# Talking-heads attention and a SoLU layer: scores of two heads on row halves of TensorE's array, the first mixing of two units on its quarters

## The chip, the core and the metric

The kernel runs on one core of a Trainium2 chip. The core has TensorE (PE in the profile; PEld is its loading of weights), VectorE (DVE), ScalarE (ACT), GpSimd (POOL) and SyncE (SP), which here only issues DMAs. The metric is the device time of one execution in microseconds, lower is better. It was 733.37 us as the median of three runs (726.63 to 737.01).

## What is computed

```python
# q, k, v: (4, 12, 448, 64); w_pre, w_post: (12, 12)
scores = q @ k.T / 8                                  # (b, h, i, j)
scores = einsum('bhij,hg->bgij', scores, w_pre)       # first mixing, over the heads
attn = softmax(scores, axis=j)
attn = einsum('bhij,hg->bgij', attn, w_post)          # second mixing
x = (attn @ v).transpose(0, 2, 1, 3).reshape(1792, 768)
h = x @ w_in                                          # (1792, 1024)
out = layernorm(h * softmax(h)) * g_ln @ w_out        # (1792, 768)
```

Every fp32 operand of the scores and of the first mixing is held as two fp16 halves, hi and lo, and three of the four products are summed: hi hi, hi lo and lo hi. The second mixing and the product with v run in fp32.

## The kernel before

**Units and blocks.** One batch has 448 rows of scores for each of 12 heads. They are cut into four blocks of rows: three of 120 rows, which are 12 units, and one of 88 rows, which is 9 units. A unit is ten rows of all heads, so 120 partitions. There are 180 units, 45 for each batch, and 16 blocks.

**Scores (`qk`, L473 to L480).** For each block and head, two matmuls of 448 columns, both over 128 rows of contraction. K lies transposed with hi above lo (`k1`), Q with lo above hi (`q2`), and the first matmul gives lo hi + hi lo at once. The second needs hi hi alone, so a copy `q1` holds the hi half of Q on the right 64 partitions and zeros on the others. `move_hi` (L458) fills it with two DMAs per two pairs of heads, from the transposed tile, and `clear_q1` sets its zeros at the start. `score_hi` on ACT and `score_lo` on DVE take each head's bank out of PSUM as fp16 hi and lo into `s` (two buffers).

**From block to unit (`fetch`, L506).** When all twelve heads of a block are out, one DMA per unit (210 KB) on SP's queue brings ten rows of all heads into the 120 partitions of `sr` (three buffers).

**First mixing (`premix`, L511).** Three matmuls of 120 x 120 x 448 with a block-diagonal weight (`wp_hi` twice, `wp_lo` once) into one of three banks (`m`). Then `rowmax` (DVE, L520), `expo` (ACT, L532), the reciprocal (DVE), `weigh` (POOL, L553), `postmix` (fp32, eight matmul instructions, L561), and `post_out` (ACT, L226) into the ring `p_t`. For each block two groups `av` (L601) of 48 instructions form attn times v, with 64 output columns each, so that two heads go to the two column halves of the array; `x_hi` (ACT) and `x_lo` (DVE) split the result.

**Next batch.** K and Q of batch b+1 are loaded, their maxima taken, split (`pair_hi` mostly on POOL, `pair_lo` on DVE or POOL, L397 to L409) and turned by transposing DMAs (`turn_in`, L411) while batch b is worked on. All of it lands on the same engines and on SP's queue.

**Order.** `Plan` is a list scheduler that runs when the program is built. Each task has an engine, a cost, a due time and rings of buffers, and the plan writes the instructions of each engine in one fixed order. On the chip each engine follows its order and waits where an operand is late. Behind attention, from about 486 us on, come the 14 tiles of the SoLU layer, which the change doesn't touch.

## Time and profile before

| | us | share of the span |
|---|---|---|
| median of three runs | 733.37 | |
| shortest, longest run | 726.63, 737.01 | |
| span of the profiled execution | 726.0 | |
| PE busy | 659.8 | 91% |
| DVE busy | 495.6 | 68% |
| ACT busy | 449.7 | 62% |
| POOL busy | 275.4 | 38% |
| premix matmuls (540) | 100.5 + 64.1 | |
| score matmuls (384) | 107.4 | |
| mean granted clock of TensorE | 0.979 | |

The span runs from the first to the last instruction of the profiled execution, and it is 0.6 us below the shortest run. The busy time of a matmul counts it from its start to its end, and matmuls overlap, so how long TensorE needs for a piece of work is read better from the distance between two starts.

### The profile page before, as it was taken

To read this page: it belongs to the slowest core of one execution; us is meant where nothing else is said; L and a number is where in the kernel's file an instruction comes from. 1 tells how busy PE (TensorE), PEld (TensorE's weight loads), DVE (VectorE), ACT (ScalarE), POOL (GpSimd) and SP (SyncE) were. 2 spreads that over 40 slices of the span, in tenths; PEclk is the share of its full clock that TensorE was granted. 3 is DMA by queue.
4 is the path that set the end of the run, shared out by engine and by line. 5 is a ranking of instruction groups with operands and counts; after the bars stand their busy time and mean duration, and the time that the engine had idled before them with its cause. 6 is when DMAs were issued, how large, how long until landed. Compare 5 with 4: busy or idle time off the path is not lost.

```text
span 726.0 us, 14785 instructions
## 1 busy us (share of the span) xinstructions
PE 659.8 (91%) x5206; PEld 479.6 (66%) x5206; DVE 495.6 (68%) x1482; ACT 449.7 (62%) x956; POOL 275.4 (38%) x384
## 2 busy tenths in 40 slices
PE   3487998999997999999999989999998848999998
PEld 2346887888886878877888878774443424566664
DVE  6777996688985778996779999848888764200000
ACT  2567787787786787788788778744555544321111
POOL 6404781134851124771113353603667622320000
PEclk9789999999999999999999999999999989999999
DMA  8736497247577347677256645536456312243112
GB/s 228 121 90 199 136 221 212 84 135 228 180 198 200 87 105 213 199 209 212 95 180 204 212 153 188 139 98 187 121 121 151 68 20 51 51 103 95 44 44 65
DMA packets 121473, 102.47 MB, mean 141 GB/s; under 512 B 75524, under 2 KB 112056, under 8 KB 121400
## 3 DMA queue, kind: packets, MB, share of 16 engines
q1 hardware_dynamic: 115128, 87.07, 43.0%
q0 software_dynamic: 4384, 12.40, 6.4%
q10 hardware_dynamic: 1888, 2.07, 1.0%
q8 instruction: 41, 0.67, 0.4%
q14 instruction: 32, 0.26, 0.1%
HBM read 33.24 MB, written 9.63 MB: 59 GB/s over the span
## 4 chain that ended last, share of the span: by engine, by line
PE 61%; DVE 14%; DMA 11%; POOL 5%; ACT 3%; issue 2%; SPq 2%; DVEq 0%; POOLq 0%; ACTq 0%
PE po L561 15%; PE y L1314 14%; PE pm L515 12%; PE ps L480 9%; PE px L601 8%; DMA sr<-s 7%; PE ps_h L764 3%; DVE cv_wo L699 2%; POOL wo L702 2%; DVE cv_wo L694 1%; DMA raw_q<-in_q_dram 1%; DVE u L1257 1%; DVE wi L222 1%; DVE wo_l L222 1%; DMA q<-q 1%
## 5 line engine op out<-in xcount | busy, mean ns | idle before, releaser
L561 PEld LDWEIGHTS po<-wr,e 120*112 120x112 f32 x1440 | 173.5, 177 | 19.0 <-POOL wr L553 6.3
L561 PE MATMUL po<-wr,e 120*112 120x120 f32 x1440 | 178.6, 267 | 2.9 <-POOL wr L553 2.8
L553 POOL TENSOR_SCALAR wr<-wq,sm 120x120 f32<-120x120 f32 x180 | 78.0, 434 | 257.6 <-DVE sm L549 117.3
L532 ACT ACTIVATE e<-pm,nb,c_exp 120x448 f32<-120x448 f32 x180 | 131.4, 731 | 15.0 <-DVE e L520 9.5
L520 DVE TENSOR_SCALAR_CACHE_REDUCE e<-pm,c_nexp 120x448 f32<-120x448 f32 x180 | 121.2, 676 | 22.2 <-PE pm L515 12.5
L491 DVE SCALAR_TENSOR_TENSOR s<-ps,s 120x448 f16<-120x448 f32 (+1 forms) x192 | 116.9, 618 | 20.3 <-ACT s L486 17.9
L226 ACT COPY p_t<-po 112x480 f32<-112x480 f32 x180 | 104.0, 578 | 32.8 <-PE po L561 31.3
L486 ACT ACTIVATE s<-ps 120x448 f16<-120x448 f32 (+1 forms) x192 | 104.0, 548 | 28.1 <-PE ps L480 20.7
L515 PE MATMUL pm<-sr,wp_hi 120*120 120x448 f16 x360 | 100.5, 361 | 17.9 <-DMA sr<-s 16.8
L480 PE MATMUL ps<-k,q 128*120 128x448 f16 (+1 forms) x384 | 107.4, 366 | 7.8 <-DVE s L491 3.5
L764 PE MATMUL ps_h<-wi,xf 128*128 128x512 f16 x396 | 87.5, 379 | 3.7 <-DVE u L1257 3.6
L1314 PE MATMUL y<-wo_h,lth 128*128 128x384 f16 (+2 forms) x224 | 72.7, 331 | 9.9 <-ACT wo_h L217 9.9
L601 PE MATMUL px<-p_t,raw_v 112*64 112x120 f32 (+1 forms) x1536 | 80.7, 261 | 0.0
L601 PEld LDWEIGHTS px<-p_t,raw_v 112*64 112x64 f32 x1536 | 73.8, 137 | 8.7 <-issue 3.1
L1314 PE MATMUL y<-wo_l,lth 128*128 128x384 f16 (+2 forms) x224 | 72.7, 331 | 2.5 <-DVE wo_l L222 2.0
L1314 PEld LDWEIGHTS <-lth 128*128 128x128 f16 x448 | 44.3, 99 | 43.9 <-issue 15.3
L1314 PE MATMUL y<-wo_h,ltl 128*128 128x384 f16 (+2 forms) x224 | 72.8, 331 | 0.0
L764 PEld LDWEIGHTS <-xf 128*128 128x128 f16 x396 | 38.5, 98 | 49.2 <-issue 4.5
L515 PEld LDWEIGHTS <-wp_hi 120*120 120x120 f16 x360 | 43.2, 134 | 34.4 <-DMA sr<-s 19.9
L480 PEld LDWEIGHTS <-q 128*120 128x120 f16 (+1 forms) x384 | 47.8, 134 | 26.7 <-issue 10.4
L515 PE MATMUL pm<-sr,wp_lo 120*120 120x448 f16 x180 | 64.1, 356 | 0.0
L1322 ACT ACTIVATE o<-y,c_out 128x384 f32<-128x384 f32 (+2 forms) x28 | 16.1, 578 | 72.4 <-PE y L1314 72.4
(168 smaller groups left out, 820.6 us busy)
## 6 DMA issues: line engine op xcount, KB each, us to landing
sr<-s SPq DMA_DIRECT2D x180, 210.0 KB
cv_wi<-in_moe_w_in_dram SPq DMA_DIRECT2D x24, 256.0 KB
cv_wo<-in_moe_w_out_dram SPq DMA_DIRECT2D x8, 768.0 KB
raw_k<-in_k_dram POOLq DMA_DIRECT2D x18, 224.0 KB, 4.4
raw_q<-in_q_dram POOLq DMA_DIRECT2D x18, 224.0 KB, 4.2
raw_v<-in_v_dram POOLq DMA_DIRECT2D x18, 224.0 KB, 3.6
q<-q SPq DMA_DIRECT2D x18, 112.0 KB
xh<-xsh SPq DMA_DIRECT2D x9, 224.0 KB
```

What stands on the lines that cost most here:

```text
L226: nc.scalar.copy(out=out, in_=in_)
L480: nc.tensor.matmul(y, x[:, e, i0 : i0 + n], k1[b, g][:, e], start=(a == 0), stop=(a == 1))
L486: nc.scalar.activation(out=s_t[b, c][0 : y.shape[0], h, 0], in_=y, func=AF.Copy, scale=2.0**-E_S)
L491: nc.vector.scalar_tensor_tensor(out=t[:, h, 1], in0=y, scalar=2.0**-E_S, in1=t[:, h, 0], op0=ALU.mult, op1=ALU.subtract)
L515: nc.tensor.matmul(ps[:, 0:S], w[0:UK], x[:, z], start=(a == 0), stop=(a == 2))
L520: nc.vector.tensor_scalar(out=e, in0=pmx[b, u][:, 0:S], scalar1=c_nexp[0:UK, b : b + 1], scalar2=None, op0=ALU.mult, op1=ALU.min, accum_ou ...
L532: nc.scalar.activation(out=ee[b, u], in_=pmx.pop((b, u))[:, 0:S], func=AF.Exp, bias=nbs.pop((b, u)), scale=c_exp[0:UK, b : b + 1], accum_o ...
L553: ENG[eng].tensor_scalar(out=w, in0=wq[0:UK, 0 : H * UN], scalar1=sums.pop((b, u)), scalar2=1.0, op0=ALU.mult, op1=ALU.mult)
L561: nc.tensor.matmul(ps[:, c * 120 : (c + 1) * 120], e[:, c * CP : (c + 1) * CP], w, start=True, stop=True)
L601: nc.tensor.matmul(xps[b, blk, g][e * 64 : e * 64 + 64, i, 0:n], raws["v", b][:, h, c * D : (c + 1) * D], block_view(b, blk, c * H + h), s ...
L764: nc.tensor.matmul(ps[:, n], xx[:, kc, o : o + 128], ww[:, kc, n * 512 : (n + 1) * 512], start=(kc == 0 and a == 0), stop=(kc == KDM - 1 a ...
L1314: nc.tensor.matmul(y, xx[:, kc], ww[:, kc, cut], start=(kc == 0 and a == 0), stop=(kc == KFF - 1 and a == 2),)
```

## The change

Scores are now made for two heads at a time. The fp16 halves are laid out by pairs: both heads' hi (128 columns) and both heads' lo, so that after the transpose one head lies on partitions 0 to 63 and the other on 64 to 127. Six matmuls of 64 rows, three for each head in turn, write two banks. `q1`, `clear_q1` and `move_hi` are gone. A block's matmuls give 128 rows now, and `fetch` picks its 120 or 88 from them. `pair_lo` on DVE is two instructions of 256 elements in place of one of 512.

The first mixing takes two units at a time. `sr` has room for both, on partitions 4 to 123, so that five rows of each unit lie on either half. Twelve matmuls of 64 x 64 write two banks: bank j gets the j-th half of both units. Where a block has nine units the last goes alone, with three matmuls as before. There are three `sr` buffers for two units each. The weights lie in 128 columns, with four partitions of zeros ahead, and all tiles behind have 128 partitions. `post_out` puts the rows back in order by its access pattern.

```diff
-    def qk(b, c, h):
-        i0, n = ROW0[b][c], ROWS[b][c]
-        for a, x in enumerate((q2[b, g], q1[g])):
-            nc.tensor.matmul(y, x[:, e, i0 : i0 + n], k1[b, g][:, e], start=(a == 0), stop=(a == 1))
+    def qk(b, c, p):
...
+        for a, (x, z) in enumerate(((0, 0), (0, 1), (1, 0))):
+            for e in range(2):
+                w = slice(64 * e, 64 * e + 64)
+                nc.tensor.matmul(
+                    sps[b, c, 2 * p + e],
+                    q2[b, g][w, j, x, i0 : i0 + QCH],
+                    k1[b, g][w, j, z],
+                    start=(a == 0),
+                    stop=(a == 2),
+                )
...
     def premix(b, u):
-        ps = pmx[b, u] = ps_m.tile([UK, 512], F32, tag="m", name=f"pm_{b}_{u}")
-        x = sr[b, u]
+        x, us = sr[b, u], mates(b, u)
+        ps = [ps_m.tile([UK, 512], F32, tag="m", name=f"pm_{b}_{n}")[:, 0:S] for n in us]
         for a, (w, z) in enumerate(((wp_hi, 0), (wp_hi, 1), (wp_lo, 0))):
-            nc.tensor.matmul(ps[:, 0:S], w[0:UK], x[:, z], start=(a == 0), stop=(a == 2))
...
+            for i in range(2):
+                for j in range(2):
+                    q, m = slice(64 * j, 64 * j + 64 - K0 * j), slice(64 * i, 64 * i + 64)
+                    nc.tensor.matmul(ps[j][m], w[q, 0, m], x[q, i, z], **kw)
...
-                        add(
-                            ("q1", b, p),
-                            one(move_hi, b, p, m),
-                            {"act": 0.1 * m} if z else {"sp": 0.6 * m},
...
-                        ring="o" if spare(b, c, h) else "s",
-                        until=[("sl", b, c, h)],
+                            ring="o" if spare(b, c, p) else "s",
+                            until=[[("sl", b, c, h + e)] for e in range(2)],
+                            slots=2,
...
+        for w in (wp_hi, wp_lo, wq):
+            nc.gpsimd.memset(w, 0.0)
+        for w in srs:
+            nc.gpsimd.memset(w[0:K0], 0.0)
...
         else:
-            split_lo(lo, x, s, hi)
+            for h in range(2):
+                split_lo(lo[:, h], x[:, h], s, hi[:, h])
```

**TensorE, second batch, units 4 and 5.** Before (ps are scores, pm the first mixing, po the second, the first number of a name is the batch):

```order
L561 MATMUL po_1_0_2121<-wr_1_0_2040,e_1_0_1994 112x120 x4
L480 LDWEIGHTS q_1_2_1463
L480 MATMUL ps_1_1_8_2130<-k_1_2_1446,q_1_2_1463 120x448
L480 LDWEIGHTS q1_2_127
L480 MATMUL ps_1_1_8_2130<-k_1_2_1446,q1_2_127 120x448
L515 LDWEIGHTS wp_hi_71
L515 MATMUL pm_1_4_2136<-sr_1_4_2023,wp_hi_71 120x448
...
L515 LDWEIGHTS wp_lo_72
L515 MATMUL pm_1_4_2136<-sr_1_4_2023,wp_lo_72 120x448
L561 MATMUL po_1_1_2142<-wr_1_1_2067,e_1_1_2021 112x120 x4
```

The same place of the change, where px is attn times v:

```order
L644 MATMUL px_0_3_0_2249<-p_t_129,raw_v0_261 64x120 x24
L491 LDWEIGHTS q_1_1_1508
L491 MATMUL ps_1_1_6_2290<-k_1_1_1498,q_1_1_1508 128x448
L491 LDWEIGHTS q_1_1_1508
L491 MATMUL ps_1_1_7_2291<-k_1_1_1498,q_1_1_1508 128x448
...
L552 LDWEIGHTS wp_hi_96
L552 MATMUL pm_1_4_2299<-sr1_94,wp_hi_96 64x448
L552 LDWEIGHTS wp_hi_96
L552 MATMUL pm_1_5_2300<-sr1_94,wp_hi_96 64x448
...
L598 MATMUL po_1_1_2318<-wr_1_1_2279,e_1_1_2185 112x120 x4
L598 MATMUL po_1_2_2327<-wr_1_2_2283,e_1_2_2228 112x120 x4
```

Six score matmuls of two heads and twelve of the first mixing of two units now stand together, and two second mixings follow each other. The places where one matmul has another tile shape (whole array, column halves, row halves, quarters) than the one before it rise from 64 to 330 in the whole program.

**SyncE's queue at the end of the first batch.** Before (sr are fetches, k and q the transposes, q1 the moves of `move_hi`):

```order
L419 DMA_TRANSPOSE q_1_1_1326<-hl_q1_1103 128x16x112
L419 DMA_TRANSPOSE k_1_1_1355<-hl_k1_886 128x16x112
L509 DMA sr_0_28_1378<-s_0_2_736 120x1x896
L509 DMA sr_0_29_1393<-s_0_2_736 120x1x896
L464 DMA q1_1_126<-q_1_1_1326 64x896 x2
L419 DMA_TRANSPOSE k_1_2_1446<-hl_k1_886 128x16x112
L509 DMA sr_0_30_1457<-s_0_2_736 120x1x896
L419 DMA_TRANSPOSE q_1_2_1463<-hl_q1_1103 128x16x112
L509 DMA sr_0_31_1482<-s_0_2_736 120x1x896
L509 DMA sr_0_32_1491<-s_0_2_736 120x1x896
L464 DMA q1_2_127<-q_1_2_1463 64x896 x2
L509 DMA sr_0_33_1535<-s_0_3_1145 120x1x896
```

And with the change:

```order
L529 DMA sr0_93<-s_0_2_818 120x1x896 x2
L529 DMA sr1_94<-s_0_2_818 120x1x896 x2
L436 DMA_TRANSPOSE k_1_1_1498<-hl_k1_899 128x16x112
L436 DMA_TRANSPOSE q_1_1_1508<-hl_q1_1160 128x16x112
L436 DMA_TRANSPOSE k_1_2_1578<-hl_k1_899 128x16x112
L436 DMA_TRANSPOSE q_1_2_1594<-hl_q1_1160 128x16x112
L529 DMA sr2_95<-s_0_3_1240 120x1x896 x2
```

The moves are gone, the last fetches of block 2 stand ahead of the last four transposes, and those follow each other without a fetch between.

**GpSimd at the start.** Before:

```order
L296 AFFINE_SELECT mk_118<-mk_118 128x10 x2
masks.py:197 MEMSET ident_70 128x128
masks.py:199 AFFINE_SELECT ident_70<-ident_70 128x128
L456 MEMSET q1_0_125 128x1792
L1131 CAST ident32_69<-ident_70 128x128
L456 MEMSET q1_1_126 128x1792
```

And with the change:

```order
L305 AFFINE_SELECT mk_121<-mk_121 128x10 x2
L314 TENSOR_TENSOR mk5_122<-mk_121 128x5
L316 MEMSET wp_hi_96 128x256
L316 MEMSET wp_lo_97 128x256
L316 MEMSET wq_98 128x128
L318 MEMSET sr0_93 4x1792
L318 MEMSET sr1_94 4x1792
L318 MEMSET sr2_95 4x1792
masks.py:197 MEMSET ident_70 128x128
masks.py:199 AFFINE_SELECT ident_70<-ident_70 128x128
L1168 CAST ident32_69<-ident_70 128x128
```

The clearing of the zeros now stands ahead of the identity matrices, of which `ident32` is an operand of the first maximum over partitions.

## Rows read from the trace of the kernel before

**Rows 1.** Page, part 4: the chain that ended last, by engine
```profile
PE 61%; DVE 14%; DMA 11%; POOL 5%; ACT 3%; issue 2%; SPq 2%; DVEq 0%; POOLq 0%; ACTq 0%
```

**Rows 2.** Windows by block: stretch, length, busy PE, PEld, DVE, ACT, POOL, clock, DMA
```profile
66.50:93.36 26.86, 26.25 (x257) 22.41 (x257) 25.47 (x90) 21.86 (x52) 18.97 (x32) 1.00 0.48 155
...
151.19:179.28 28.09, 26.80 (x255) 23.18 (x254) 23.69 (x83) 21.77 (x51) 12.47 (x24) 1.00 0.62 194
...
206.42:240.56 34.14, 29.93 (x258) 24.45 (x257) 22.18 (x75) 24.77 (x60) 8.07 (x14) 0.95 0.76 196
...
369.94:396.67 26.73, 26.73 (x254) 23.09 (x253) 23.39 (x73) 22.82 (x51) 7.90 (x13) 1.00 0.61 199
...
426.61:455.12 28.51, 26.83 (x250) 22.23 (x249) 26.93 (x80) 23.06 (x52) 12.83 (x15) 1.00 0.61 195
...
sum 439.23, PE 415.91 PEld 348.98 DVE 360.44 ACT 341.62 POOL 180.79; mean PE 25.99 PEld 21.81 DVE 22.53 ACT 21.35 POOL 11.30
```

**Rows 3.** Timeline of PE: start, time, line, operation, shape, count
```profile
143.33 0.54 PE L515 MATMUL pm<-sr,wp_hi 120*120 120x448 f16 x2
...
143.90 0.98 PE L561 MATMUL po<-wr,e 120*112 120x120 f32 x8
144.72 0.54 PE L480 MATMUL ps<-k,q 128*120 128x448 f16 x2
145.10 0.98 PE L561 MATMUL po<-wr,e 120*112 120x120 f32 x8
...
157.07 0.54 PE L480 MATMUL ps<-k,q 128*120 128x448 f16 x2
157.54 2.68 PE L601 MATMUL px<-p_t,raw_v 112*64 112x120 f32 x48
160.15 0.59 PE L480 MATMUL ps<-k,q 128*120 128x448 f16 x2
```

**Rows 4.** Groups by line and form: DVE's splits and its score step
```profile
L491 DVE SCALAR_TENSOR_TENSOR s<-ps,s 120x448 f16<-120x448 f32 x144 | 87.7, 618 | 10.2 <-ACT s L486 8.8 <-DMA sr<-s 0.2
...
L222 DVE SCALAR_TENSOR_TENSOR xsl<-px,x_sc,xsh 128x120 f16<-128x120 f32 x72 | 20.1, 333 | 14.6 <-ACT xsh L217 14.4
...
L222 DVE SCALAR_TENSOR_TENSOR hl_q<-raw_q,p_q,hl_q 112x512 f16<-112x512 f32 x20 | 15.6, 788 | 0.2 <-ACT hl_q L217 0.2
```

**Rows 5.** Chain in order of time, start of the program: start, time, what
```profile
25.77 4.08 DMA q<-hl_q
29.93 6.37 DMA q<-q
36.34 3.92 PE ps L480 x11
42.78 3.85 DMA sr<-s
...
58.74 7.71 DMA sr<-s
```

**Rows 6.** Timeline of SP's queue at the start: the last transpose of Q
```profile
29.92 1.69 SPq L419 DMA_TRANSPOSE q<-hl_q  x1
```

**Rows 7.** Timeline, second batch boundary: SP's queue and the PE behind it
```profile
227.41 2.04 SPq L464 DMA_DIRECT2D q<-q  x2
...
229.50 1.64 SPq L419 DMA_TRANSPOSE q<-hl_q  x1
...
231.24 1.78 SPq L509 DMA_DIRECT2D sr<-s  x2
...
234.11 0.88 PE L515 MATMUL pm<-sr,wp_hi 120*120 120x448 f16 x2 [3.76 <-DMA sr<-s]
```

**Rows 8.** Waits, longest in total: us, times, longest
```profile
PE pm L515 <- DMA sr<-s: 16.8, 14, 3.8
```

**Rows 9.** Timeline, GpSimd at the start and the first use of `ident32`
```profile
4.01 1.59 POOL L456 MEMSET q<- 128x1792 f16 x1
...
5.54 0.29 POOL L1131 CAST ident<-ident 128x128 f32<-128x128 f16 x1
...
9.64 0.77 PE L189 MATMUL spread_k<-ident,amx_k 128*128 128x128 f32 x2 [9.64 <-DVE amx_k L210]
```

More of the change, by code (lines that the diff above doesn't have):

```diff
@@ L29, in __init__, with add @@
         self.tasks = {}
-    def add(self, key, run, on, after=(), behind=(), due=0.0, ring=None, until=(), lat=0.0):
+        self.slots = {}
+    def add(self, key, run, on, after=(), behind=(), due=0.0, ring=None, until=(), lat=0.0, slots=None):
+        if slots:
+            self.slots[key] = slots
         self.tasks[key] = (run, on, list(after), due, ring, list(until), lat, list(behind))
@@ L279 @@
     mk = const.tile([128, UN], F32, name="mk")
+    mk5 = const.tile([128, HN], F32, name="mk5")
     am_w = const.tile([128, 2], F32, name="am_w")
@@ L795, in add_tasks @@
             last = ("mix", i)
-        for g in range(NPAIR // GP):
-            add(("cl", g), one(clear_q1, g), {"pool": 1.6}, due=3.0 + g)
         turns = ([(p, GP) for p in range(0, NPAIR, GP)], [(0, 1), (1, 1), (2, 1), (3, 1), (4, 1), (5, 1)])
@@ L956, in add_tasks @@
                     due=d - 2 * STEP,
-                    ring="sr",
-                    until=[("m",) + g],
+                    ring="sr" if u == mates(b, u)[0] else None,
+                    until=[M(b, u)],
                     lat=2.7,
                 )
-                add(
-                    ("m",) + g,
-                    one(premix, *g),
-                    {"pe": 0.56},
-                    after=[("f",) + g, last] + behind("m"),
-                    due=d,
-                    ring="m",
-                    until=[("ex",) + g],
-                )
+                us = mates(b, u)
+                if u == us[0]:
+                    add(
+                        ("m",) + g,
+                        one(premix, *g),
+                        {"pe": 0.66},
+                        after=[("f", b, n) for n in us] + [last] + [M(*p) for p in [prev] if u or b],
+                        due=d,
+                        ring="m",
+                        until=[[("ex", b, n)] for n in us],
+                        slots=len(us),
+                    )
                 add(
@@ L1053, in add_tasks @@
                         {"sp": 0.65},
-                        after=[("xl", b, NBLK[b] - 1, g) for g in range(NXG)] + [("m", b + 1, 8 + i)],
+                        after=[("xl", b, NBLK[b] - 1, g) for g in range(NXG)] + [M(b + 1, 8 + i)],
                         due=at(b + 1, 10 + i),
@@ L1065, in add_tasks @@
                 {"sp": 0.65},
-                after=[("xd", b, j) for b in range(2) for j in range(XP)] + [("m", o, 28 + 2 * i)],
+                after=[("xd", b, j) for b in range(2) for j in range(XP)] + [M(o, 28 + 2 * i)],
                 behind=[("x0", i - 1)] if i else [],
```

176 lines of the change are left out of this document (99 added, 77 removed).

## The prediction

> **What bounds the kernel now.** The chain that ended last comes first: TensorE holds 61% of it, DVE 14%, DMA 11% [rows 1]. The change touches attention alone, so I cut attention into its 16 blocks, each from its first `premix` to that of the next: together 439.2 us for 180 units, 2.44 us a unit [rows 2]. The reader is to see two kinds of block there. In most, PE is busy nearly throughout and DVE and ACT for some 80 to 85% (151.19, 369.94). In five of them, 60 units, of which 66.50 and 426.61 are the first and the last, DVE is busy for 94% and more (25.47 of 26.86, 26.93 of 28.51): there the split of the next K and Q, or of the weights of the last layer, fills it.
>
> How long TensorE needs is read from the distance of two starts [rows 3]. From 143.33 to 143.90 three premix matmuls take 0.57 us, 0.19 each. From 143.90 to 144.72 a postmix takes 0.82. From 144.72 to 145.10 one head's scores take 0.38. A group of `av` takes 2.61, from 157.54 to 160.15. A block of 12 units needs 12 x (0.57 + 0.82 + 0.38) + 2 x 2.61 = 26.5 us, and the block at 369.94 took 26.73 [rows 2]. So outside the five, TensorE is the bound.
>
> **Term 1: TensorE's work.** Scores now cost 192 x 0.38 = 73.0 us and premixes 180 x 0.57 = 102.6, together 175.6. After it, two heads are three steps of 448 columns if the two row halves run at once, and two units are three steps if the four quarters do. With 0.19 a step that is 96 x 0.57 + 88 x 0.57 + 4 x 0.57 (units left alone) = 107.2, so 68.4 less. Whether halves and quarters run at once no row shows for rows of the array. For columns one does: 48 instructions of `av` would need 48 x 0.1025 = 4.92 us at the pace of postmix (0.82 / 8, the same 120 columns in fp32), and took 2.61, so two column halves did run together [rows 3]. I take the same for rows.
>
> Against this stands the change of tile shape. The scores at 157.07 are followed by `av` after 0.47 us, where others need 0.38 [rows 3]: entering column halves costs 0.09. Leaving them costs at most 2.61 - 24 x 0.1025 = 0.15. The order has 330 such changes where it had 64. At 0.09 for each of the 266 more, that is 24 us and leaves 44.5, or 0.25 us a unit. Bounds: 179 more entries at 0.09 with a free return leave 52 (0.29 a unit); with 0.15 for each return they leave 25 (0.14 a unit).
>
> The Trainium skill ("TensorE: Matmul & The Clock Gate", Measured speedup vs the span model) speaks against the full overlap: four row tiles of 512 columns gave 3.07x and not 4x. By that a step would take 0.19 x 4 / 3.07 = 0.25 us, an estimate, and TensorE would save 175.6 - (552 steps x 0.25 + 2.3 + 24), some 11 us in place of 44.5. The pair of column halves in this trace reached 4.92 / 2.61 = 1.88 of 2, with the return from them inside that number, so I stay with the row.
>
> **Term 2: what of it reaches the end.** In the five blocks that DVE fills I count nothing. In the other eleven, 120 units, TensorE is the bound until the next engine is: 120 x 0.25 = 30 us. The next engine stands near: the block at 369.94 has DVE busy for 23.39, which at the 95% of the full blocks is 24.6 us, so it can give 2.1 of its 3.0. I count **-29** (bounds -17 and -35).
>
> **Term 3: the start.** The first fetch leaves at 42.78, because the scores waited for `move_hi`: a transposed tile lands 4.08 us after 25.77, the move issued at 29.93 needs 6.37 more, and eleven matmuls follow [rows 5]. Without moves the last transpose, issued at 29.92 [rows 6], lands near 34, and two heads on ACT and DVE (0.62 each on DVE [rows 4]) end at about 37. So block 0 can start 5 to 6 us earlier. It doesn't all last: block 1 waits for its own scores (its fetch at 58.74 needed 7.71 us [rows 5]), and a pair of heads now holds both banks until both are out, about 0.66 + 3 x 0.62 (ACT's first half, then DVE's two) and the waits between, near 2.7 us, or 16 us for six pairs, as long as the 16 us from 42.78 to 58.74. GpSimd clears its zeros ahead of `ident32`. With 1.59 us for each clearing of 1792 elements [rows 9], were four partitions to cost as much as 128, `ident32` would come at about 10 in place of 5.54, and its first use stood at 9.64, so up to 0.5 us later. I take **-2.5** (0 to -6).
>
> **Term 4: SP's queue.** At the second batch boundary two moves hold the queue for 2.04 us, a transpose for 1.64, and only then the fetch goes at 231.24 for which TensorE waits 3.76 us [rows 7]. Without 18 moves such a fetch leaves earlier; but four transposes now stand in a row without a fetch. Three boundaries of this kind can hold at most 3 x 3.76 = 11 of the 16.8 us for which its matmuls waited for fetches [rows 8]. I take a third, **-3.8** (0 to -11).
>
> **Term 5: DVE's splits.** The order has 68 splits of 256 elements on DVE where it had 33 of 512. From 120 elements (333 ns) to 512 (788 ns) [rows 4] the fixed part is 0.19 us and 256 elements cost 0.49: 68 x 0.49 - 33 x 0.79 = 7.4 us more at most, 4 if two behind each other overlap as other DVE instructions do. They lie mostly in the blocks that DVE fills, where nothing hides them. **+4.5** (0 to +7.4).
>
> **Term 6: pairs wait for two.** A premix waits for two fetches and for two of the three banks. SP issues a fetch every 0.89 us (1.78 for two [rows 7]), and TensorE waits 14 times for a fetch [rows 8], so at most 14 x 0.89 = 12. With three double buffers I take **+2** (0 to +12). The bank cycle of a pair (premix, two `rowmax`, one `expo`) is far below two units.
>
> **Sum.** -29 - 2.5 - 3.8 + 4.5 + 2 = -28.8 us. The profiled span is 726.0, 0.6 below the shortest run and 7.4 below the median. So the span becomes 697, and the median, if it keeps that distance, **705 us**.
>
> **Rivals.**
>
> *Reading PSUM is the bound everywhere.* ACT and DVE take every score and every mixing out of PSUM, as many instructions as before. DVE's 360 and ACT's 342 of 439 us [rows 2] would fill 82% and 78%; if dependences between them allow no more, TensorE's gain turns into waiting, and only terms 3 to 6 remain: about 733, no change. For it: five blocks are at 94% and more. Against it: the block at 369.94 lasts as long as TensorE's work, with DVE free for 3.3 us. The Trainium skill states this rule ("TensorEngine Tiling (Array Packing)", PSUM Bottleneck): tiling speeds up TensorE, not the evacuation. The trace agrees in those five blocks.
>
> *The row halves run one after the other.* Then the change doesn't do what it says: a pair of scores is 6 x 0.19 = 1.14 where two heads took 0.76 (+36 us), a pair of premixes stays at 1.14, and the changes of shape add 24. TensorE gets 60 us more and bounds all blocks: 726 + 60 - 6 + 7.4, about **787 us**, slower. No row shows row halves; that the column halves do overlap speaks against it. It turns slower once a step takes over (173.3 - 24) / 552 = 0.27 us in place of 0.19.
>
> *All blocks gain.* With a free return from halves, and the splits moved to where DVE is idle, all 180 units gain 0.29: -52 - 6 - 7.6 + 4 = -61.6, about **672 us**. Against it: DVE's 360 us leave little room at 385.
>
> **How the numbers follow.** Forecast 0.60 (its own range 692 to 718), PSUM-bound 0.23 (719 to 736), all blocks 0.08, row halves in turn 0.07, another loss above 748 0.02. A change of 2%, 14.7 us, is about what a measurement of this kernel can tell from none, so faster means under 718.7: 0.60 + 0.08 = 0.68; same 0.23; slower 0.09. The range 686 to 731 holds the forecast and most of the second rival, and leaves out the last two and most of the third, under 2 in 10.
>
> **What would show it.** Right: score matmuls of a pair start in twos, and from a pair's first matmul to the next task 0.57 to 0.75 us pass; a premix of two units likewise in place of 1.14; blocks such as the one at 369.94 shrink to 24 us, those of 66.50 and 426.61 stay at 26 to 29; the first fetch leaves near 38; no move stands on SP's queue. Wrong: pairs at 0.9 us and more (the steps don't overlap, or a change of shape costs far more than 0.09); TensorE idle for ACT or DVE in blocks where DVE is under 90%; new waits for a second fetch at block starts; or DVE blocks that grow by more than 2 us.

## The result and the profile after

The changed kernel takes 735.38 us (median of 20 runs, 729.93 to 742.22), the kernel before 731.17 in the same session: a ratio of 1.0065, 95% interval 1.0040 to 1.0089. It is slower by some 5 us, less than the 2% that decides a verdict, and 30 us above the forecast.

The page of the changed kernel, span, busy times, and the chain that ended last by engine, which answers to [rows 1]:

```profile
span 730.6 us, 16210 instructions
...
PE 648.0 (89%) x5926; PEld 415.7 (57%) x5926; DVE 505.9 (69%) x1517; ACT 453.1 (62%) x956; POOL 266.9 (37%) x390
...
PE 49%; DVE 24%; ACT 8%; DMA 8%; POOL 6%; issue 3%; SPq 0%; ACTq 0%; POOLq 0%; DVEq 0%
```

TensorE's part of the chain fell from 61% to 49%, DVE's rose from 14% to 24%: more of the end now passes through the other engines.

The timeline of PE (start, time, line, operation, shape, count) in a full stretch, which answers to [rows 3]:

```profile
140.66 0.57 PE L552 MATMUL pm<-sr,wp_hi 64*64 64x448 f16 x8
141.06 0.36 PE L552 MATMUL pm<-sr,wp_lo 64*64 64x448 f16 x4
141.35 1.07 PE L598 MATMUL po<-wr,e 128*112 128x120 f32 x8
142.35 0.74 PE L491 MATMUL ps<-k,q 64*128 64x448 f16 x6
143.03 1.07 PE L598 MATMUL po<-wr,e 128*112 128x120 f32 x8
...
145.90 0.57 PE L552 MATMUL pm<-sr,wp_hi 64*64 64x448 f16 x8
146.30 0.36 PE L552 MATMUL pm<-sr,wp_lo 64*64 64x448 f16 x4
146.59 0.74 PE L491 MATMUL ps<-k,q 64*128 64x448 f16 x6
```

The premix of two units takes 0.69 us (140.66 to 141.35) in place of 1.14, the scores of two heads 0.67 or 0.68 (142.35 to 143.03) in place of 0.76. Halves and quarters do run at once. The postmix between them takes 1.00 (141.35 to 142.35) where it took 0.82.

Windows by block, which answer to [rows 2] (stretch, length, busy PE, PEld, DVE, ACT, POOL, clock, DMA); the first is block 0:

```profile
42.18:70.35 28.17, 23.61 (x209) 14.41 (x210) 19.23 (x59) 17.20 (x39) 7.93 (x16) 0.82 0.55 157
...
125.46:151.85 26.39, 25.23 (x299) 18.39 (x298) 19.96 (x75) 22.80 (x53) 4.42 (x13) 1.00 0.27 101
181.18:213.26 32.08, 25.93 (x281) 18.77 (x281) 30.73 (x93) 18.98 (x44) 22.95 (x35) 0.95 0.44 148
213.26:243.72 30.46, 29.01 (x323) 20.42 (x323) 22.48 (x83) 27.78 (x66) 5.64 (x15) 1.00 0.88 181
243.72:264.14 20.42, 20.42 (x252) 15.16 (x251) 15.34 (x55) 16.64 (x39) 3.21 (x9) 1.00 0.35 87
264.14:292.09 27.95, 24.98 (x324) 18.40 (x322) 22.69 (x73) 20.81 (x50) 10.94 (x22) 1.00 0.59 168
372.40:399.23 26.83, 24.59 (x295) 17.70 (x295) 22.22 (x79) 23.41 (x55) 5.03 (x12) 1.00 0.52 173
431.89:459.42 27.53, 24.61 (x296) 18.15 (x296) 26.03 (x77) 22.56 (x50) 10.50 (x14) 1.00 0.61 175
```

The two blocks of nine units with which a batch begins (46.77 and 265.31), a block that DVE fills (179.28) and the last block of the second batch (240.56) stood so in the kernel before:

```profile
46.77:66.50 19.73, 14.97 (x86) 10.89 (x86) 14.22 (x45) 12.54 (x30) 7.26 (x14) 0.92 0.64 172
...
179.28:206.42 27.14, 27.14 (x257) 23.35 (x256) 25.65 (x83) 21.79 (x50) 21.39 (x35) 1.00 0.55 179
...
240.56:265.31 24.75, 23.49 (x224) 19.63 (x223) 17.98 (x59) 19.50 (x47) 3.62 (x10) 1.00 0.30 73
265.31:285.31 20.00, 20.00 (x216) 17.36 (x215) 16.95 (x55) 15.29 (x38) 8.77 (x17) 1.00 0.64 183
```

The block that I took as the sign for TensorE's gain needs 26.83 us, as before (26.73 in [rows 2]), but TensorE has 2.2 us free in it. The two short blocks are 8 us longer each; the block ahead of the second one is 4.3 shorter (24.75 to 20.42). Attention lasts from 42.18 to 492.0, 449.8 us in place of 441.3; its start is 4.6 earlier; what follows it takes 238.6 in place of 237.9.

Windows over all sixteen blocks of both traces close the account: -4.6 at the start, +16.4 in the two first blocks, +4.9 in the five blocks that DVE filled, -12.7 in the other nine, +0.7 behind attention, together 4.7 where the spans differ by 4.6. So the nine did get shorter on the whole; the loss stands in the two first blocks and in those of DVE.

The granted clock over attention (the last but two of the columns) was lower too, 0.99 before and then 0.97:

```profile
46.77:488.06 441.29, 417.97 (x3913) 350.87 (x3914) 360.44 (x1163) 341.62 (x786) 180.79 (x299) 0.99 0.57 170
```

```profile
42.18:492.00 449.82, 407.56 (x4623) 289.29 (x4624) 370.01 (x1190) 346.42 (x787) 171.53 (x298) 0.97 0.58 159
```

Waits of PE in the kernel before and then in the changed one, in total, times, longest (with [rows 8]):

```profile
PE po L561 <- POOL wr L553: 2.8, 5, 0.9
...
PE pm L515 <- ACT e L532: 0.7, 2, 0.4
```

```profile
PE pm L552 <- ACT e L569: 11.4, 13, 2.4
...
PE po L598 <- POOL wr L590: 9.2, 15, 1.7
...
PE pm L552 <- DMA sr<-s: 8.2, 7, 1.8
```

Premixes wait 8.2 us for fetches in place of 16.8, and 11.4 for `expo` on ACT, that is, for a bank, in place of 0.7; postmixes wait 9.2 for weights in place of 2.8.

### The profile page after: what moved, and what is told of

Its sections match the earlier page's. It is cut to its first block, busy times and chain, and to the rows that moved or that the text cites. A ratio compares the mean times of both kernels' runs of the same rounds, so it can differ in the third digit from the quotient of the medians.

```text
span 730.6 us, 16210 instructions
## 1 busy us (share of the span) xinstructions
PE 648.0 (89%) x5926; PEld 415.7 (57%) x5926; DVE 505.9 (69%) x1517; ACT 453.1 (62%) x956; POOL 266.9 (37%) x390
## 4 chain that ended last, share of the span: by engine, by line
PE 49%; DVE 24%; ACT 8%; DMA 8%; POOL 6%; issue 3%; SPq 0%; ACTq 0%; POOLq 0%; DVEq 0%
PE y L1351 14%; PE po L598 13%; PE px L644 8%; PE ps L491 6%; PE pm L552 5%; DMA sr<-s 4%; DVE s L508 4%; ACT e L569 4%; DVE e L557 3%; PE ps_h L807 3%; DVE hl_q L229 2%; POOL wo L745 2%; DVE cv_wo L742 2%; DMA raw_q<-in_q_dram 2%; ACT s L503 2%
## 5 line engine op out<-in xcount | busy, mean ns | idle before, releaser
L598 PE MATMUL po<-wr,e 128*112 128x120 f32 x1440 | 186.0, 278 | 12.5 <-POOL wr L590 9.2
L598 PEld LDWEIGHTS po<-wr,e 128*112 128x112 f32 x1440 | 161.7, 180 | 59.1 <-POOL wr L590 30.8
L590 POOL TENSOR_SCALAR wr<-wq,sm 128x120 f32<-128x120 f32 x180 | 71.0, 396 | 257.7 <-DVE sm L586 172.2
L569 ACT ACTIVATE e<-pm,nb,c_exp 128x448 f32<-128x448 f32 x180 | 131.6, 733 | 29.4 <-DVE e L557 17.8
L557 DVE TENSOR_SCALAR_CACHE_REDUCE e<-pm,c_nexp 128x448 f32<-128x448 f32 x180 | 119.7, 677 | 18.5 <-PE pm L552 14.5
L508 DVE SCALAR_TENSOR_TENSOR s<-ps,s 128x448 f16<-128x448 f32 x192 | 115.0, 618 | 14.7 <-ACT s L503 12.9
L503 ACT ACTIVATE s<-ps 128x448 f16<-128x448 f32 x192 | 99.6, 549 | 26.8 <-PE ps L491 25.3
L491 PE MATMUL ps<-k,q 64*128 64x448 f16 x576 | 80.8, 371 | 12.2 <-DVE s L508 5.5
L644 PEld LDWEIGHTS px<-p_t,raw_v 112*64 112x64 f32 x1536 | 73.9, 137 | 10.7 <-ACT p_t L233 4.0
L552 PE MATMUL pm<-sr,wp_hi 64*64 64x448 f16 x704 | 62.0, 374 | 20.0 <-ACT e L569 11.4
L1351 PEld LDWEIGHTS <-lth 128*128 128x128 f16 x448 | 44.6, 100 | 43.7 <-issue 15.7
L229 DVE SCALAR_TENSOR_TENSOR xsl<-px,x_sc,xsh 128x120 f16<-128x120 f32 (+1 forms) x104 | 27.0, 318 | 19.5 <-ACT xsh L224 18.9
```

Source lines behind the costliest of these rows:

```text
L491: nc.tensor.matmul(sps[b, c, 2 * p + e], q2[b, g][w, j, x, i0 : i0 + QCH], k1[b, g][w, j, z], start=(a == 0), stop=(a == 2),)
L503: nc.scalar.activation(out=s_t[b, c][0 : y.shape[0], h, 0], in_=y, func=AF.Copy, scale=2.0**-E_S)
L508: nc.vector.scalar_tensor_tensor(out=t[:, h, 1], in0=y, scalar=2.0**-E_S, in1=t[:, h, 0], op0=ALU.mult, op1=ALU.subtract)
L552: nc.tensor.matmul(ps[j][m], w[q, 0, m], x[q, i, z], **kw)
L557: nc.vector.tensor_scalar(out=e, in0=pmx[b, u][:, 0:S], scalar1=c_nexp[0:UK, b : b + 1], scalar2=None, op0=ALU.mult, op1=ALU.min, accum_ou ...
L569: nc.scalar.activation(out=ee[b, u], in_=pmx.pop((b, u))[:, 0:S], func=AF.Exp, bias=nbs.pop((b, u)), scale=c_exp[0:UK, b : b + 1], accum_o ...
```

## The experiments

Theory A: TensorE sets the end, and its changes of shape ate the gain. Theory B: pairs wait for two banks and two fetches. Theory C: DVE sets the end. Theory D came later: too few units can be under way. Ratios are to the kernel before, run in the same session, with 95% intervals; 0.001 is 0.73 us.

| kernel | ratio | interval |
|---|---|---|
| the change | 1.0065 | 1.0040 to 1.0089 |
| e1 scores alone | 1.0214 | 1.0143 to 1.0286 |
| e2 mixing alone, small buffers | 1.0483 | 1.0405 to 1.0561 |
| e2c the change, small buffers | 1.0268 | 1.0208 to 1.0327 |
| e3 scores as pairs, whole array | 1.0066 | 1.0029 to 1.0102 |
| e4 the change, third step out | 1.0038 | 1.0002 to 1.0074 |
| e4b before, third step out | 0.9853 | 0.9799 to 0.9907 |
| e5 the change, guard out | 1.0023 | 0.9988 to 1.0057 |
| w2 another order | 1.0023 | 0.9994 to 1.0052 |
| e6 mixing pairs on the whole array | 1.0208 | 1.0158 to 1.0257 |
| k1 filler in block 0 | 1.0039 | 1.0008 to 1.0069 |
| xa another order | 1.0042 | 1.0007 to 1.0077 |
| xb before, another order | 1.0011 | 0.9973 to 1.0049 |
| e1b scores alone, six ahead | 1.0047 | 1.0014 to 1.0081 |
| n6 the change, six buffers | 0.9833 | 0.9786 to 0.9880 |
| n6x six buffers, new order | 0.9660 | 0.9614 to 0.9705 |
| s6 scores alone, six ahead, six buffers | 1.0016 | 0.9986 to 1.0045 |
| n6e4 six buffers, third step out | 0.9802 | 0.9742 to 0.9861 |
| n4x four buffers, the new order | 0.9979 | 0.9949 to 1.0010 |

### The two parts apart: e1, e2, e2c, e3

e1 makes every unit its own task again (the plan is told 0.56 us for it):

```diff
 def mates(b, u):
-    c = block_of(b, u)
-    u -= (u - BLK0[b][c]) % 2
-    return list(range(u, min(u + 2, BLK0[b][c + 1])))
+    return [u]
```

> The change's scores (two heads on row halves), but the first mixing unit by unit with three matmuls of the whole array, one bank and one buffer for each unit. Theory A, changes of tile shape: a visit of TensorE to a pair of scores costs 0.67 us and some 0.3 around it where two heads took 0.76, so 96 visits lose 10 to 20 us of its work, less 4 us of the earlier start: 735 to 745. Theory B, pairs that hold two banks: the scores of a block come out later whatever their shape; the 9-unit blocks at the start of a batch, which took 28 us in the change and 20 before, stay near 28, and the time is about as in A. Theory C, the mixing is to blame: 725 to 729, faster than before by the earlier start.

e2 keeps the pairs of mixings and takes scores, transposes and moves from the kernel before; it has room for two pairs of fetches and three exponentials only (`NE`; the expectations call them tiles of row maxima). e2c is the change with these small buffers, its control:

```diff
-    NE, NWR = 4, 3
+    NE, NWR = 3, 3
-    AHEAD = 3
+    AHEAD = 2
```

> The change's first mixing (two units on the quarters), but the scores head by head with their copy of the hi half, as before. To fit into the memory it has two double buffers for fetches in place of three, and three of the row-maximum tiles in place of four; e2c shows what that costs. Theory A: 88 visits of 0.69 and some 0.3 around it for 1.14 save 10 to 15 us of TensorE's work, so it is faster than e2c by 8 to 15 us. Theory B for the scores' banks: the 9-unit blocks fall back from 28 to 20 us, and it is faster than e2c by 10 to 20 us. Theory C, the mixing's pairs are to blame: as slow as e2c.

> The change whole, with the two smaller buffers of e2: two double buffers for fetches and three tiles of row maxima. Control for e2. If fetches ahead or these tiles are what TensorE waits for, it is slower than the change by over 10 us; if not, within 5 us of it.

e3 is the kernel before with the scores of two heads as one task, on the whole array:

```diff
+    def qk2(b, c, h0):
+        i0, n = ROW0[b][c], ROWS[b][c]
+        pool, tag = (ps_o, "o") if spare(b, c, h0) else (ps_s, "s")
+        for h in (h0, h0 + 1):
+            ps = pool.tile([128, 512], F32, tag=tag, name=f"ps_{b}_{c}_{h}")
+            sps[b, c, h] = ps[0:n, 0:S]
+        for a in range(2):
+            for h in (h0, h0 + 1):
+                g, e = divmod(h, 2 * GP)
+                x = (q2[b, g], q1[g])[a]
+                nc.tensor.matmul(sps[b, c, h], x[:, e, i0 : i0 + n], k1[b, g][:, e], start=(a == 0), stop=(a == 1))
```

> The kernel before, with only this: the scores of two heads are one task that takes both banks at once (four matmuls of the whole array, head by head in turn). No halves, no change of tile shape, the same matmuls. Theory A: nothing lost, 731 within 3 us. Theory B: the pair holds two banks until both heads are out, blocks of 9 units at the start of a batch grow from 20 to 25 us and more, and the time rises by 8 to 16 us.

Measured: e3 735.22, e1 747.81, e2c 750.92, e2 769.70. Tying the scores in pairs costs 4.8 us without any tile (e3). Smaller buffers cost the change 15 us (e2c). Either part alone is slower than both together, which none of the theories foresaw. Block 0 goes with the scores' pairs: it takes 26.89 us in e3 and 20.61 in e2, which makes the scores head by head, as theory B had it (19.73 in the kernel before, 28.17 in the change). First e3, then e2:

```profile
46.63:73.52 26.89, 23.44 (x126) 16.99 (x127) 18.30 (x58) 16.23 (x37) 7.34 (x16) 0.81 0.48 135
```

```profile
45.67:66.28 20.61, 15.47 (x128) 10.34 (x128) 15.48 (x47) 13.72 (x33) 7.28 (x14) 1.00 0.70 181
```

The first block of the third batch doesn't follow it: 21.3 in e3 and 27.6 in e2, so its extra time goes with the mixings' pairs or with their order. e1 had a fault as a control, seen only later: its three fetch buffers hold three units, where the change's three hold three pairs, six units. Its premixes waited 19.3 us for fetches:

```profile
PE pm L545 <- DMA sr<-s: 19.3, 20, 4.5
```

### What TensorE's and DVE's time are worth: e4, e4b, e5, e6

e4 leaves out the low part of the weights in the first mixing, with the order of the change as it is; e4b does so in the kernel before; e5 leaves out the guard of the sums:

```diff
-        for a, (w, z) in enumerate(((wp_hi, 0), (wp_hi, 1), (wp_lo, 0))):
-            kw = dict(start=(a == 0), stop=(a == 2))
+        for a, (w, z) in enumerate(((wp_hi, 0), (wp_hi, 1))):
+            kw = dict(start=(a == 0), stop=(a == 1))
```

```diff
-            nc.vector.tensor_scalar(out=sm, in0=sm, scalar1=1e-9, scalar2=None, op0=ALU.add)
+            pass
```

> The changed kernel with the third of the three steps of the first mixing left out (low part of the weights times high part of the scores), in the order of the changed kernel: 88 x 0.19 + 4 x 0.19 = 17 us less for TensorE, the changes of tile shape and everything else as they were. Theory A (TensorE still sets the end; its shape changes ate what the halves gave): about three quarters of the 17 us show, some 722 us. Theory B (pairs wait for two banks and two fetches; TensorE idles for them): nearly nothing shows, 731 to 736 us. Theory C (DVE sets the end): nothing shows, 733 to 736 us.

> The kernel before with the same third step of the first mixing left out: 180 x 0.19 = 34 us less for TensorE and no other edit. It tests the premise of the prediction that TensorE sets the pace of eleven blocks of sixteen in the kernel before. If it does: 120 units x 0.19 = 23 us show, some 708 us. If waits for other engines stand right behind TensorE (theories B and C in the kernel before already): under 10 us, 722 us or more.

> The changed kernel without the 180 short instructions on DVE that add 1e-9 to the sums of the exponentials (left out of the computation): 180 x about 0.1 to 0.19 us, some 18 to 34 us less on DVE, and each unit's chain shorter by about as much. Theory C (DVE sets the end): 15 us or more show, 720 us or less. Theory A (TensorE): 0 to 4 us, 731 us or more. Theory B (bank and fetch waits): 0 to 5 us, since the bank of a mixing is free before this instruction runs.

Measured: 34 us less on TensorE make the kernel before 10.7 us faster (0.9853), 31% of the cut (20 to 43% by the interval) and not the two thirds that its expectation counted. 17 us less make the change 2.0 us faster, a difference inside the intervals; 17 us less on DVE (busy 489.2 in place of 505.9) make it 3.1 faster, about as much as they leave open. So neither engine alone sets the end, in the kernel before already not TensorE alone. In e4b the block that answers to 369.94 takes 25.89 in place of 26.73, though its twelve premixes need 2.3 us less:

```profile
365.39:391.28 25.89, 25.12 (x242) 21.31 (x241) 23.21 (x73) 22.22 (x51) 7.98 (x13) 1.00 0.65 208
```

e6 gives each unit of a pair the whole array, with the order and the waits of the change:

```diff
-            for i in range(2):
-                for j in range(2):
-                    q, m = slice(64 * j, 64 * j + 64 - K0 * j), slice(64 * i, 64 * i + 64)
-                    nc.tensor.matmul(ps[j][m], w[q, 0, m], x[q, i, z], **kw)
+            for i in range(2):
+                nc.tensor.matmul(ps[i], w[0 : KS.stop, 1], x[0 : KS.stop, i, z], **kw)
```

> The changed kernel, every engine's order of tasks as it is, with one edit: the first mixing of two units is still one task that waits for two fetches and two banks, but each unit has the whole array (three matmuls of 0.19 us and then three). TensorE's work grows by 88 x (1.14 - 0.69) = 40 us and shrinks by the changes of shape that go, at most 176 x 0.09 = 16: net 24 us more or above. Theory A (TensorE's time sets the end): 20 us more, some 755 us. Theory B (the waits of pairs set it, and TensorE has slack): under 8 us more, 735 to 743 us.

Its timeline of PE shows a pair at 1.14 us (141.53 to 142.67), and the postmix behind it, which has whole-array work ahead and a score pair behind, at 0.92 (142.67 to 143.59):

```profile
141.53 0.92 PE L550 MATMUL pm<-sr,wp_hi 124*128 124x448 f16 x4
...
142.67 0.99 PE L596 MATMUL po<-wr,e 128*112 128x120 f32 x8
143.59 0.74 PE L491 MATMUL ps<-k,q 64*128 64x448 f16 x6
```

It takes 745.25, 10.5 us more than the change by the ratios, above theory B's range and below theory A's 755. The work added is more than the 24 us of the expectation: in the order only 44 of the changes of shape go (238 to 194, counted in the order), since score pairs stand beside many of the mixings, so it is 39.6 - 44 x 0.09 = 36 us, and 29% of it comes out. That is the share of e4b. e4's 12% is lower, but its interval reaches 5 us, 30%.

### Whether the order or the clock did it: w2, xa, xb, k1

w2, xa and xb order the same instructions otherwise; their edits are numbers that the plan is told. The main ones of w2 (`SWITCH` written shorter):

```diff
-    SWITCH = {("m", "o"): 0.087, ("av", "o"): 0.073, ("m", "av"): 0.057, ("o", "qk"): 0.04, ("o", "m"): 0.026}
+    SWITCH = {(a, b): 0.1 for a in ("m", "qk", "o", "av") for b in ("m", "qk", "o", "av") if a != b}
-            free[e] = t + on[e] + 0 * self.SWITCH.get((last.get(e), k[0]), 0)
+            t = t + (0.15 if (last.get(e), k[0]) in self.SWITCH else 0)
+            free[e] = t + on[e]
-                    due = at(b, u0 - 6) - STEP * 0.6 * (H - h)
+                    due = at(b, u0 - 4) - STEP * 1 * (H - h)
...
-                        {"pe": 0.66},
+                        {"pe": 0.57},
```

> The changed kernel with another order of the same instructions: the plan is told 0.57 us for a pair of mixings, 0.66 for a pair of scores and 0.15 more for each change between kinds of task on TensorE (before it 0.66, 0.66 and 0), and the scores of a block fall due evenly over twelve units in place of seven. Changes of shape grow from 336 to 358. Theory A alone (the price of the changes): 22 changes more at 0.15, 735 to 739 us. Theory B (a pair holds both banks, and pairs that come close together wait for each other, so that what counts is where they stand): 8 to 16 us gained, 719 to 727 us.

> The changed kernel with another order again: scores due evenly over twelve units, mixings due half a unit later, fetches due one unit ahead in place of two, 0.09 us told for each change between whole array and parts of it, spacing of the due times 2.5 in place of 2.25. If the order decides where the pairs' waits fall (theory B): 8 to 14 us less than the changed kernel, 721 to 727 us. If TensorE's longer pairs and changes of shape set the end (theory A): 730 us or more.

> The kernel before with another order of the same instructions: scores due one unit earlier, and 0.09 us told for each change into and out of the column halves. A control for what an order alone is worth: if orders scatter by several us whatever the kernel, 722 to 728 us, and differences of that size between kernels with different orders say nothing of shapes and banks; if the order of before is as good as it gets, 729 to 733 us.

Measured 730.94, 733.68 and 732.02. These orders move either kernel by 1 to 3 us, hardly more than the intervals. (The traces count 330 changes of shape in the change and 350 in w2, where the expectation has 336 and 358.) So none of these orders finds the 30 us.

k1 lets 40 filler matmuls in place of 10 run from the tenth head of scores on (`range(40 + 10)` becomes `range(40 + 40)`):

> The changed kernel with 40 in place of 10 of the matmuls without a result that fill TensorE's free time from the tenth head of scores on. In the changed kernel TensorE stands nearly idle from 40 to 44 us and its clock is granted at half from 44 to 54. If that costs the start: with filler the clock stays at 1.0 there, block 0 shortens by 2 to 5 us, some 731 us. If the scores of the next block set the length of block 0 and not TensorE's pace: no change, or a loss of up to 4 us where filler stands ahead of work, 735 to 739 us.

Windows in block 0, of the change and then of k1:

```profile
46.00:50.00 4.00, 3.17 (x21) 1.50 (x18) 2.91 (x10) 2.46 (x7) 1.70 (x3) 0.50 0.52 133
50.00:54.00 4.00, 4.00 (x30) 2.08 (x30) 1.52 (x8) 3.05 (x7) 2.69 (x5) 0.62 0.78 214
```

```profile
46.00:50.00 4.00, 3.44 (x31) 1.73 (x29) 3.13 (x13) 2.80 (x9) 1.89 (x4) 1.00 0.62 157
50.00:54.00 4.00, 3.57 (x37) 2.54 (x37) 2.81 (x10) 3.08 (x8) 1.87 (x5) 1.00 0.84 223
...
42.58:70.13 27.55, 22.42 (x225) 14.50 (x224) 20.02 (x61) 16.95 (x39) 7.99 (x16) 1.00 0.54 154
```

The filler holds the granted clock at 1.00 (2.4 GHz) where it was at 0.50 (1.2 GHz) and 0.62, and block 0 still takes 27.55 us. The clock did not make it long. The whole gained 1.9 us, inside the intervals.

### Units under way: e1b, n6, n6x, s6, n6e4, n4x

A unit holds an exponential buffer from its `rowmax` to the end of its `postmix`, and the plan places no `rowmax` before a buffer is free. There are four. n6 makes them six, and the weights' buffers four, in the space that `q1` left:

```diff
-    NE, NWR = 4, 3
+    NE, NWR = 6, 4
```

e1b repeats e1 with six units fetched ahead (`AHEAD = 6`, tiles of one unit). n6x is n6 with an order for it: spacing `STEP` 2.5, scores due at `u0 - 7` with a factor of 0.9, premixes half a unit and postmixes a unit later, a price of 0.09 for each change between the whole array and parts, and 0.69 for a pair of scores.

> The changed kernel with six buffers for the exponentials in place of four and four for the weights of the second mixing in place of three, in the space that the moved copies of Q left free. A unit holds an exponential buffer from its row maximum on DVE to the end of its second mixing on TensorE. Theory D (with four of them, two pairs are all that is under way, and a pair waits for the last second mixing but one): the waits of first mixings for ACT and of second mixings for the weights shrink, 8 to 12 us less than the changed kernel, 724 to 728 us. Theory B (the banks of pairs, which stay as they are) and theory A (TensorE's time): 732 to 737 us.

> The same with six buffers, and with an order that lets the second mixings fall due a unit later, spreads the scores over eleven units and is told 0.09 us for each change between the whole array and parts of it. Theory D: the deeper buffers need such an order to be used, 715 to 724 us. Theory A or B: 730 us or more, as the two orders tried before on four buffers gave.

> The kernel with the scores in pairs and the first mixing unit by unit (e1), with fetch buffers for six units ahead in place of three. The changed kernel holds three pairs, six units, where the kernel before and e1 hold three units. If this depth is what made the changed kernel faster than e1: 735 to 740 us. If it is the four quarters: 745 to 750 us, as e1.

Measured: n6 720.25 (0.9833), n6x 707.63 (0.9660), e1b 734.95 (1.0047). Theory D's numbers came out better than it expected; with e1b the depth of fetches explains e1: 12 us of its loss were the three units, and scores alone with six ahead are as fast as both parts.

The last three complete the squares. s6 is e1b with the buffers of n6; n6e4 is n6 without the third step; n4x is n6x with `NE, NWR = 4, 3`:

> Scores in pairs on row halves, first mixing unit by unit on the whole array, six units fetched ahead (e1b), and six buffers for the exponentials and four for the weights as in the run with six buffers. It differs from that one by the four quarters alone. If TensorE's work counts once the buffers are there (the quarters take 102.6 us to 63 and add changes of shape): 726 to 735 us. If buffers for exponentials are all: 718 to 723 us.

> The changed kernel with six buffers for the exponentials, and the third step of the first mixing left out of the computation: 17 us less for TensorE in the order of the run with six buffers. With four buffers the same cut gave 2.8 us. If the buffers stood in front of TensorE's gain (theory D): 8 to 12 us less than 720, some 708 to 712 us. If not: 716 to 720 us.

> The settings of the order of the run with six buffers and a new order (707.6 us), with four buffers for the exponentials and three for the weights. It tells the order from the buffers. If the buffers are what the order uses (theory D): 728 to 736 us, as the changed kernel and the two orders tried on it. If the order alone did it: 710 to 722 us.

| | four buffers | six buffers |
|---|---|---|
| scores alone, six ahead | 1.0047 | 1.0016 |
| scores and quarters | 1.0065 | 0.9833 |
| scores and quarters, order of n6x | 0.9979 | 0.9660 |

With four buffers the quarters bring nothing (1.0047 to 1.0065). With six they bring 13 us (1.0016 to 0.9833), 37% of the 36 us that e6 counts for them on TensorE. Six buffers bring scores alone 2 us, scores and quarters 17, and with the order of n6x 23. Either alone is worth nothing that can be measured; both together are. The order gives 6 us with four buffers and 13 with six.

n6e4 missed: 17 us less of TensorE give 2.3 us with six buffers (at most 8 by the intervals), where D expected 8 to 12. So this cut doesn't show the limit back at TensorE: at most half of it comes out. The granted clock stands in the way of a finer reading: it was 0.962 in the profiled run of n6e4 and 0.971 in that of n6, by estimate 0.009 x 714 = 6 us of TensorE at full clock, so the cut may be worth more than it shows. Waits of PE, first n6, then n6x:

```profile
PE po L598 <- POOL wr L590: 10.9, 18, 2.1
...
PE pm L552 <- DMA sr<-s: 6.4, 4, 2.4
PE pm L552 <- ACT e L569: 6.0, 6, 2.3
```

```profile
PE po L599 <- POOL wr L591: 6.3, 12, 1.4
...
PE pm L553 <- ACT e L570: 2.2, 5, 0.8
PE pm L553 <- DMA sr<-s: 2.0, 3, 1.1
```

Waits for a bank fall from 11.4 to 6.0 and 2.2, those for fetches from 8.2 to 6.4 and 2.0. Those for weights, which theory D expected to shrink, rise from 9.2 to 10.9 in n6 and fall to 6.3 in n6x only. Blocks of n6x, by windows; that of 123.13 answers to the change's fourth block (26.39 us), that of 405.92 to 431.89 above:

```profile
123.13:146.47 23.34, 23.30 (x286) 16.80 (x285) 18.84 (x72) 20.76 (x50) 4.65 (x13) 1.00 0.28 107
...
405.92:430.50 24.58, 23.85 (x290) 17.82 (x289) 23.91 (x76) 21.65 (x48) 11.31 (x14) 1.00 0.64 193
```

Each is 3 us shorter, and TensorE, DVE and ACT are each busy for a larger share of it. Of the 10.7 us by which attention is shorter in n6 than in the change, 7.3 lie in the five blocks that DVE filled and 4.3 in the other nine; the two first blocks stay as long as they were (27.72 and 29.25). So the buffers didn't give back what those blocks lost; they gained elsewhere.

Theory D's mechanism, too few units under way, isn't shown. A unit counts as under way from the start of its `rowmax` to the end of its `postmix`; the shares are of the time from the first start to the last end. Two or fewer were under way for 9% in the kernel before and for 27% in the change (four for 37% and 28%), which agrees with pairs that make the number swing. But in n6 two or fewer still were for 26%, five or six for 8% only, and s6, with more units under way than n6 (3.45 on average against 3.09), is the slower of the two. In n6x five or six were for 24%. Nor do the waits of DVE show it: `rowmax` waited for a `postmix`, that is, for an exponential buffer, for 1.9 us in all in the change, less than before. The kernel before, then the change:

```profile
DVE e L520 <- PE po L561: 6.1, 8, 2.3
```

```profile
DVE e L557 <- PE po L598: 1.9, 6, 0.6
```

The buffers can act on the order as well: where one would not be free in the plan, it puts the `rowmax` later.

n6 and n6x are faster than both kernels of the comparison. Left open: n6 changed the exponentials' and the weights' buffers at once, and the plan orders anew whenever a buffer count changes, so buffer and order can't be told apart; why e1 is slower than e3, though it has no moves; and the kernel before with six buffers, for which there is no space.

## Why the prediction was wrong

**Term 1, right in kind, its size at the lower side.** Halves and quarters overlap. A pair takes 0.67 (scores) or 0.69 (premix), where 0.57 was taken: 96 x 0.67 + 88 x 0.69 + 4 x 0.57 = 127.3 us in place of 107.2. The quarters give 2.28 / 0.69 = 3.30 of 4, the halves 1.14 / 0.67 = 1.70 of 2. The Trainium skill ("TensorE: Matmul & The Clock Gate", Measured speedup vs the span model) has 3.07 for four row tiles. By its figure, an estimate of 0.25 a step, a pair would take 0.75, nearer than my 0.57. The price of a change was about right: a postmix with tiled work on both sides takes 0.18 more, 0.09 for each side. But fewer count than the 330: quarters followed by halves pay nothing more (145.90 to 146.59 is 0.69 again). If column halves behind other parts are free too, which I didn't read, the order has 238 that pay where it had 64, 174 x 0.09 = 15.7 us. TensorE's work falls by 175.6 - 127.3 - 15.7 = 32.6 us and not 44.5, within the bounds. The sum is for the full clock; I had no term for the lower granted clock of the change (0.97 over attention, 0.99 before), and k1 tells what it costs in block 0 alone.

**Term 2, the step that failed.** I let TensorE's gain reach the end in eleven blocks of sixteen, because its work filled them. e4b prices that premise: 31% of a cut reaches the end. So 32.6 us are worth 10 and not 29. The windows agree: nine of the eleven blocks became 12.7 us shorter together, with term 4's 3.7 among them, which leaves 9. What I read as "TensorE is the bound" looks like an engine that takes about as long as the chains through the others: in e4b the block of 369.94 gave back 0.8 of 2.3 us. PE busy nearly throughout [rows 2] doesn't tell the two apart.

**Term 6, the second step that failed; its reason is open in part.** "With three double buffers I take +2", "The bank cycle of a pair (...) is far below two units". Mixing pairs on the whole array cost 11.8 us against units one by one (e6 against e1b), score pairs 4.8 (e3): 17 together, though each is measured on its own base and order. I looked at banks and fetches and not at the exponentials' four buffers, whose count the change leaves as it is while units come by twos. Two more of them, with one more for the weights and the order that the plan made for them, turned the loss of the whole into a gain (n6). No other edit of the change did so clear of noise; n4x's 0.9979 is the nearest. But the gain lies in other blocks than the loss, and neither the waits of DVE nor the count of units shows those buffers to be what the pairs waited for.

**Term 3, the start: right, then lost in the same block.** The first fetch leaves at 38.13 (SP's queue) and the first premix starts at 42.18 (46.77 before, in the windows above); then the timeline of PE:

```profile
38.13 8.07 SPq L529 DMA_DIRECT2D sr<-s  x6
```

```profile
42.18 0.38 PE L552 MATMUL pm<-sr,wp_hi 64*64 64x448 f16 x2 [1.76 <-DMA sr<-s]
43.88 0.95 PE L552 MATMUL pm<-sr,wp_hi 64*64 64x448 f16 x6 [1.33 <-DMA sr<-s]
...
45.14 1.30 PE L491 MATMUL ps<-k,q 64*128 64x448 f16 x6
...
67.31 0.72 PE L491 MATMUL ps<-k,q 64*128 64x448 f16 x5 [0.18 <-DVE amx_k L217]
```

The pair waits 1.33 us in its middle for the second fetch. The six score pairs of the next block stand from 45.14 to 67.31, 22 us and not the 16 that I estimated, so the next block begins at 70.35 in place of 66.50: -4.6 became +3.9. Six buffers don't shorten block 0 (27.56 us in n6x), nor does the clock (k1). It is as long with pairs of scores on the whole array (e3) and short again without pairs (e2), so its length comes from the pairs of scores and where they stand, not from the tiles. The first block of the third batch (264.14) loses 8 us as well, 4.3 of them gained in the block ahead of it, and not with the scores' pairs (e3); n6x has it at 23.74, and what it waits for stays open.

**Term 4, right at its place.** No move stands on SP's queue, and the block at the second batch boundary takes 30.46 in place of 34.14, -3.7 where -3.8 was counted for all.

**Term 5, too small, and on the whole of little weight.** DVE's groups of the split, of the kernel before for K and then of the change:

```profile
L222 DVE SCALAR_TENSOR_TENSOR hl_k<-raw_k,p_k,hl_k 112x512 f16<-112x512 f32 x13 | 14.4, 1109 | 0.0
```

```profile
L229 DVE SCALAR_TENSOR_TENSOR hl_q<-raw_q,p_q,hl_q 112x256 f16<-112x256 f32 x40 | 26.0, 696 | 0.2 <-ACT hl_q L224 0.2
...
L229 DVE SCALAR_TENSOR_TENSOR hl_k<-raw_k,p_k,hl_k 112x256 f16<-112x256 f32 x28 | 17.7, 678 | 0.0
```

43.7 us in place of 15.6 [rows 4] + 14.4 = 30.0: 13.7 more and not 4.5, since 256 elements take nearly as long as 512 on Q's side. By e5, 17 us of DVE are worth 3, a figure at the edge of its interval, so this term is some 2 us of the time. The signs were mixed. The block of 426.61, now at 431.89, stayed at 27.5, as foretold; that of 66.50 took 24.5 and not 26 to 29; and that of 179.28 grew from 27.14 to 32.08, one of the signs of being wrong. There 18 splits took DVE 12.3 us, where 6 had taken 4.7. So the order gathered them in that block, which the term did not count; no run tests it by itself.

**The sum, in measured sizes.** -10 (terms 1 and 2), -4.6 (start), -3.7 (SP's queue), +2 (DVE), +17 (pairs) make about +1, where +4.2 was measured. The bases differ (the pairs' price holds what the start and the short blocks lost again), so it closes only roughly; the windows by block above close without them.

**The rivals.** "Reading PSUM is the bound everywhere" had 733 us, and that is where the time came out. Its mechanism is not shown: n6x reads the same scores and mixings out of PSUM and does attention in 422 us, so 450 was no floor of ACT or DVE. What six buffers and the order made for them took away is shown by its size and not by its mechanism. "Row halves in turn" is excluded by the timeline, and "all blocks gain" by the two first blocks and the five of DVE, which grew taken together.

## What to carry to other kernels

An engine that is busy throughout a block is not yet the one that sets its length: cut some of its work on the chip, and count only the share of the cut that comes out (here about 30%). Whoever makes one task of two should look at every buffer that a task holds to the end of its chain, not only at those it waits for at its start, and count them anew; here the gain showed only when those buffers grew with the pairs, though the traces don't show why. A tile that runs at once with others also needs its own pair price and a price for each change to and from the whole array, and both are read from distances between starts.

## What the runs showed of the hardware

Four quarters of 64 rows and 64 columns, twelve matmuls of 448 columns, take 0.69 us, two row halves (six matmuls) 0.67, against 0.57 for three on the whole array. A group of eight fp32 matmuls on the whole array takes 0.82 alone, 0.92 with tiled work on one side, 1.00 with it on both; quarters and row halves behind each other show no such price. The Trainium skill ("TensorEngine Tiling (Array Packing)", Key Properties) says that a change of tiling mode drains the engine; the traces agree for changes between the whole array and parts of it, at 0.09 us each, and show no price from quarters to row halves (0.69 for the pair of premixes at 145.90 as at 140.66).

GpSimd clears four partitions of 1792 elements three times in 4.65 us, 1.55 each, as long as 128 partitions took ([rows 9], 1.59); the first use of `ident32` came at 9.99 us, 0.35 later than before.
